# Attention and a two-layer feed-forward on one core: the GpSimd library, the first memsets and the first loads rearranged

## The chip, the core and the metric

The kernel runs on one core of one Trainium2 chip. The metric is the device time of one execution in microseconds (us), the median of several runs. The engines are called as in the profile: PE is TensorE, DVE is VectorE, ACT is ScalarE, POOL is GpSimd, and SP is the engine that issues the DMAs.

## The reference

Linear attention over 8 batches, 8 heads, 576 positions and 64 columns, then a feed-forward over the 4608 tokens with 512 columns:

```python
q_s = np.exp(q - np.max(q, axis=-1, keepdims=True))
q_s = q_s / (np.sum(q_s, axis=-1, keepdims=True) + 1e-09)
k_s = np.exp(k - np.max(k, axis=2, keepdims=True))
k_s = k_s / (np.sum(k_s, axis=2, keepdims=True) + 1e-09)
kv = np.einsum('bhsd,bhse->bhde', k_s, v)
attn = np.einsum('bhsd,bhde->bhse', q_s, kv)
x = attn.transpose(0, 2, 1, 3).reshape(B * S, H * D)
h = x @ w_in                        # w_in  512 x 2048, float64
g = h * (1.0 / (1.0 + np.exp(-1.702 * h)))
out = (g @ w_out).astype(np.float32)  # w_out 2048 x 512, float64
```

The maximum of k runs over the positions, which lie across the partitions; the maximum of q runs along a row.

## The kernel before

The 4608 tokens are 12 blocks (t) of 384. For each block the kernel makes x from the attention, and then for each of 16 slices j of the hidden dimension PE runs g1 (12 matmuls, `L585`), ACT the activation, and PE g2 (9 matmuls, `L617`). The weights arrive as 64-bit words, and `conv_w` turns each of the 32 weight tiles (wi0 to wi15, wo0 to wo15) into a high and a low part, once: two instructions on ACT (`L243`, `L256`) and four on DVE (`L247`, `L251`, `L252`, `L262`), some 2.5 us of DVE a tile. Blocks 0 and 1 run interleaved, while the weights are still being turned.

The attention of batch b starts with `k_max`: DVE takes the maximum over the chunks that one partition holds (`L378`, `L379`, `L380`, the last with the 64 tail positions), and POOL takes it across the partitions (`L384`, one PARTITION_ALL_REDUCE for each group of heads). Then `k_sub` subtracts it on DVE (`L398`, `L401`) and ACT takes the exponential; `kv_pair` multiplies with v on PE (`L441`, `L442`). `q_soft` is the softmax of q (`L479` to `L489`); `q_tr` transposes it on PE with the matrix `ident`, `x_pair` gives x. Batches 0 and 1 have two groups of four heads, later batches four of two.

All DMAs of loads stand in one queue, SP's, in the order batch 0's k, tail, k, q, q, eight of v, then wi0 and wo0, then batch 1, then the other weights. Eight semaphores are shared by them in turn, so that a DMA is issued when the eighth before it has landed. Tiles of batches 0 and 1 (ek, ev, eq, et) lie in buffers that the late weights take over. A `Plan` sorts all operations into one order for each engine from ranks and estimated costs; each engine then works through its own list in order.

Before all this, POOL clears or fills tiles with memsets, makes `ident` (a memset and an AFFINE_SELECT, lines of masks.py), and runs one PARTITION_ALL_REDUCE on 64 columns of a tile mx, `warm`, `L197`. The second group's maxima are written to the same tile mx by `L379`. The AFFINE_SELECT and the PARTITION_ALL_REDUCE belong to code libraries that the program loads into POOL; the loads are instructions in POOL's list.

Of the kernel before, what the change touches and what calls it, by code (L numbers as in the profile page):

```python
# [14 lines left out]
ALU = mybir.AluOpType  # L15
# [83 lines left out]
def dve(n, psum=False):  # L99
    return 0.15 + n / 960  # L100
# [7 lines left out]
def efficient_attention_then_gelu_ffn(  # L108
# [25 lines left out]
    SM = 512  # L134
    CM = SM // P
# [10 lines left out]
    def sb(name, shape, dtype=F32, tag=None):  # L146
        return const.tile(shape, dtype, name=name, tag=tag or name)
# [14 lines left out]
    m1_ = sb("m1", [P, 2 * 4 * D])  # L162
    tail = [(sb(f"kl{i}", [P, H, D]), sb(f"vl{i}", [P, H, W])) for i in range(1)]

    for t in kvn:
        nc.gpsimd.memset(t, 0.0)
    make_identity(nc, ident)
    for t in vt_:
        nc.gpsimd.memset(t[:, :, :, D:W], 1.0)

    def zero_tail(kl, vl):
        nc.gpsimd.memset(kl[ST:P], 0.0)
        nc.gpsimd.memset(vl[ST:P], 0.0)
# [5 lines left out]
    def early(tag, name, shape):
        return sb(name, shape, tag=tag)  # L180

    ek, ev, eq, etail = {}, {}, {}, {}
    for b in range(2):
        for gr in range(2):
            ek[b, gr] = early(f"wo{15 - 4 * b - gr}", f"ek{b}{gr}", [P, CM, 4, D]), f"wo{15 - 4 * b - gr}"
            ev[b, gr] = early(f"wo{13 - 4 * b - gr}", f"ev{b}{gr}", [P, 4, CM, W]), f"wo{13 - 4 * b - gr}"
            eq[b, gr] = early(f"wi{15 - 2 * b - gr}", f"eq{b}{gr}", [P, C, 4, D]), f"wi{15 - 2 * b - gr}"
            nc.gpsimd.memset(ev[b, gr][0][:, :, :, D:W], 1.0)
    et = early("wi11", "et", [P, H * (D + W)])
    etail[0] = (  # L190
        et[:, : H * D].rearrange("p (h d) -> p h d", h=H),
        et[:, H * D : H * (D + W)].rearrange("p (h d) -> p h d", h=H),
    ), "wi11"
    zero_tail(*etail[0][0])

    def warm():
        nc.gpsimd.partition_all_reduce(mx_[0][:, 0], mx_[0][:, 0], P, bass_isa.ReduceOp.max)  # L197

    nc.gpsimd.memset(mx_[0][:, 0], 0.0)
    plan.add("POOL", 6.0, (), (("mx", 0),), -1000, warm)  # L200

    wi = [[None] * NJ for _ in range(2)]
    wo = [[None] * NJ for _ in range(2)]
# [71 lines left out]
    def bc(a, n):  # L275
        return a.unsqueeze(len(a.shape)).broadcast_to([*a.shape, n])
# [23 lines left out]

    def load_k(b, i, rank):
        n = group(b)
        if b < 2:
            t, tag = ek[b, i]
            key = (tag, 0)
        else:
            t, key = kt_[i % 2], ("kt", i % 2)
        kbuf[b, i] = t, key
        hs = slice(n * i, n * (i + 1))

        def run():
            nc.sync.dma_start(  # L312
                out=t, in_=k[b, hs, 0:SM, :].rearrange("h (p c) d -> p c h d", c=CM)
            )

        plan.add("SP", plan.ISSUE, (), (key,), rank, run, size=n * SM * D * 4)

    def load_v(b, i, rank):
        n = group(b)
        if b < 2:  # L320
            t, tag = ev[b, i]
            key = (tag, 0)
        else:
            t, key = vt_[i % 2], ("vt", i % 2)
# [19 lines left out]

    def load_q(t, i, rank):
        n = group(t)
        if t < 2:
            qt, tag = eq[t, i]
            key = (tag, 0)
        else:  # L350
            qt, key = qt_[i % 2], ("qt", i % 2)
        qbuf[t, i] = qt, key
        hs = slice(n * i, n * (i + 1))

        def run():
            for b, s0, p0, p1 in parts(t):
                nc.sync.dma_start(  # L357
                    out=qt[p0:p1], in_=q[b, hs, s0 : s0 + (p1 - p0) * C, :].rearrange("h (p c) d -> p c h d", c=C)
                )

        plan.add("SP", plan.ISSUE * len(parts(t)), (), (key,), rank, run, size=n * TB * D * 4)

# [27 lines left out]
    def k_sub(b, i, rank):  # L390
        n = group(b)
        t, key = kbuf[b, i]
        kl, _, (lkey, _) = tbuf[b]
        mx, M = maxes[b, i]
        hs = slice(n * i, n * (i + 1))

        def run():
# [10 lines left out]
        plan.add("DVE", dve(n * CM * D) + dve(n * D), (key, M, lkey), (key, L), rank, run)  # L408
# [90 lines left out]
    def q_tr(t, hp, rank):  # L499
# [152 lines left out]
    def at(rank, f, *a):  # L652
        tasks.append((rank, len(tasks), f, a))
# [37 lines left out]
    attend(1, 1, 0.4, 0.1)  # L691
    for j in range(NJ):
# [67 lines left out]
```

## Time and profile before

| | us |
|---|---|
| median of 3 runs | 939.67 (lowest 938.83, highest 940.52) |
| profiled execution, its own time | 938.21 |
| span of its trace, first to last instruction | 936.4 |
| PE busy | 895.0 (96% of the span) |
| DVE busy | 410.2 (44%) |
| ACT busy | 508.5 (54%) |
| POOL busy | 28.0 (3%) |

Times in the trace count from the span's start. The profiled execution takes 1.8 us more than its span. An engine's share over the whole span is an average: the first 75 us look different from the rest.

### The profile page before, as it was taken

To read this page: it belongs to the slowest core of one execution; us is meant where nothing else is said; L and a number is where in the kernel's file an instruction comes from. 1 tells how busy PE (TensorE), PEld (TensorE's weight loads), DVE (VectorE), ACT (ScalarE), POOL (GpSimd) and SP (SyncE) were. 2 spreads that over 40 slices of the span, in tenths; PEclk is the share of its full clock that TensorE was granted. 3 is DMA by queue.
4 is the path that set the end of the run, shared out by engine and by line. 5 is a ranking of instruction groups with operands and counts; after the bars stand their busy time and mean duration, and the time that the engine had idled before them with its cause. 6 is when DMAs were issued, how large, how long until landed. Compare 5 with 4: busy or idle time off the path is not lost.

```text
span 936.4 us, 12002 instructions
## 1 busy us (share of the span) xinstructions
PE 895.0 (96%) x4652; PEld 810.9 (87%) x4652; DVE 410.2 (44%) x904; ACT 508.5 (54%) x876; POOL 28.0 (3%) x50
## 2 busy tenths in 40 slices
PE   0689999999999999999999999999999999999998
PEld 0568999899999999999999999999999999999997
DVE  2999996174351551441562443342355243142111
ACT  1776767366483783553675566454478275352222
POOL 3000000000000000000000000000000000000000
PEclk9899999999999999999999999999999999999999
DMA  9998000030121130000230230000222110000000
GB/s 209 269 372 211 1 1 1 34 100 22 36 47 55 42 74 35 18 18 34 62 74 34 63 73 35 18 17 35 54 48 56 43 33 18 35 18 1 35 1 34
DMA packets 129241, 55.30 MB, mean 59 GB/s; under 512 B 114336, under 2 KB 122528, under 8 KB 129184
## 3 DMA queue, kind: packets, MB, share of 16 engines
q1 hardware_dynamic: 129184, 54.54, 23.2%
q8 instruction: 36, 0.59, 0.2%
q14 instruction: 21, 0.17, 0.1%
HBM read 45.09 MB, written 9.44 MB: 58 GB/s over the span
## 4 chain that ended last, share of the span: by engine, by line
PE 92%; SPq 4%; DMA 2%; DVE 1%; issue 0%; ACT 0%; DVEq 0%
PE bank L585 43%; PE bank L617 42%; PE bank L552 2%; PE bank L441 2%; PE bank L508 1%; SPq L329 1%; DMA raw<-in_moe_w_out 1%; DMA raw<-in_moe_w_in 1%; SPq L357 1%; SPq L293 1%; PE bank L442 1%; SPq L213 0%; DVE tmp L251 0%; DVE tmp L252 0%; SPq L312 0%; SPq L218 0%
## 5 line engine op out<-in xcount | busy, mean ns | idle before, releaser
L585 PE MATMUL bank<-xh,w 128*128 128x384 f32 x1536 | 429.5, 341 | 4.6 <-ACT w L256 2.7
L617 PE MATMUL bank<-w,gh 128*128 128x512 f32 x1152 | 364.1, 397 | 1.4 <-ACT gh L594 1.4
L585 PEld LDWEIGHTS bank<-xh,w 128*128 128x128 f32 x1536 | 282.1, 188 | 12.3 <-ACT w L256 3.3
L597 DVE TENSOR_TENSOR gl<-g,gh 128x384 fp32r<-128x384 f32 x192 | 106.8, 556 | 384.7 <-ACT gh L594 376.9
L585 PE MATMUL bank<-xl,w 128*128 128x384 f32 x768 | 259.6, 338 | 0.0
L591 ACT ACTIVATE g<-bank 128x384 f32<-128x384 f32 x192 | 94.3, 491 | 301.2 <-PE bank L585 300.1
L617 PEld LDWEIGHTS bank<-w,gh 128*128 128x128 f32 x1152 | 212.5, 188 | 35.8 <-ACT gh L594 1.8
L617 PE MATMUL bank<-w,gl 128*128 128x512 f32 x576 | 227.6, 395 | 3.0 <-DVE gl L597 3.0
L585 PEld LDWEIGHTS bank<-xl,w 128*128 128x128 f32 x768 | 144.6, 188 | 6.0 <-DVE xl L562 0.3
L617 PEld LDWEIGHTS bank<-w,gl 128*128 128x128 f32 x576 | 108.6, 188 | 29.0 <-DVE gl L597 4.1
L594 ACT CAST gh<-g 128x384 fp32r<-128x384 f32 x192 | 98.5, 513 | 6.2 <-PE bank L617 0.3
L591 ACT ACT_TABLE_LOAD x58 | 74.4, 1283 | 1.0
L384 POOL PARTITION_ALL_REDUCE mx<-mx x28 | 23.4, 834 | 712.3 <-DVE mx L380 712.3
L483 ACT ACT_TABLE_LOAD x33 | 42.3, 1283 | 0.6
L451 ACT ACTIVATE kvn<-bank,r 64x64 f32<-64x64 f32 x64 | 19.6, 307 | 27.9 <-DVE r L446 26.1
L441 PE MATMUL bank<-ev,ek 128*128 128x130 f32 x64 | 12.0, 346 | 23.4 <-ACT ek L404 22.9
L479 DVE TENSOR_REDUCE qm<-qt 128x6 f32<-128x384 f32 x40 | 21.9, 548 | 25.5 <-DMA qt<-in_q 25.0
L486 DVE TENSOR_REDUCE qm<-qt 128x6 f32<-128x384 f32 x40 | 22.0, 549 | 25.3 <-ACT qt L483 25.2
L404 ACT ACT_TABLE_LOAD x25 | 32.1, 1283 | 1.1 <-PEq L747 0.7
L441 PEld LDWEIGHTS bank<-ev,ek 128*128 128x128 f32 x64 | 11.0, 256 | 24.1 <-POOL mx L384 22.9
L559 ACT CAST xh<-bank 128x384 fp32r<-128x384 f32 x48 | 22.7, 475 | 12.7 <-PE bank L552 12.3
L562 DVE TENSOR_TENSOR xl<-bank,xh 128x384 fp32r<-128x384 f32 x48 | 26.1, 551 | 5.9 <-ACT xh L559 5.8
(73 smaller groups left out, 590.6 us busy)
## 6 DMA issues: line engine op xcount, KB each, us to landing
out<-tmp SPq DMA_DIRECT2D x36, 256.0 KB, 2.1
raw<-in_moe_w_in SPq DMA_DIRECT2D x16, 512.0 KB, 10.3
raw<-in_moe_w_out SPq DMA_DIRECT2D x16, 512.0 KB, 9.3
kt<-in_k SPq DMA_DIRECT2D x24, 256.0 KB, 3.5
vt<-in_v SPq DMA_DIRECT2D x48, 128.0 KB, 3.4
qt<-in_q SPq DMA_DIRECT2D x28, 192.0 KB, 3.0
qt<-in_q SPq DMA_DIRECT2D x24, 96.0 KB, 2.6
ek<-in_k SPq DMA_DIRECT2D x4, 512.0 KB, 6.0
```

The costliest lines, as they stand in the source:

```text
L384: nc.gpsimd.partition_all_reduce(flat, flat, P, bass_isa.ReduceOp.max)
L404: nc.scalar.activation(t, t, AF.Exp)
L441: nc.tensor.matmul(pk[:, :w], kt[:, c, loc, :], vt[:, loc, c, :], start=c == 0, stop=False)
L483: nc.scalar.activation(qt, qt, AF.Exp)
L486: nc.vector.tensor_reduce(out=m, in_=qt, axis=AX.X, op=ALU.add)
L559: nc.scalar.copy(xh, px[:, :TB])
L562: nc.vector.tensor_tensor(out=xl, in0=px[:, :TB], in1=xh.bitcast(F32), op=ALU.subtract)
L585: nc.tensor.matmul(ph, wi[w][j][:, c, :], x[:, c, :], start=c == 0 and i == 0, stop=c == KC - 1 and i == 2,)
L591: nc.scalar.activation(gt, ph, AF.Gelu_apprx_sigmoid)
L594: nc.scalar.copy(gh, gt)
L597: nc.vector.tensor_tensor(out=gl, in0=gt, in1=gh.bitcast(F32), op=ALU.subtract)
L617: nc.tensor.matmul(po[c], x[:, cs], wo[w][j], start=j == 0 and i == 0, stop=j == NJ - 1 and i == 2)
```

## The change

Four things are changed, all in the first microseconds. The all-reduce that makes POOL load its library works on a tile of its own, `first`, and stands at the head of POOL's list. `ident` is made behind the two all-reduces of batch 0. All other memsets at the start are issued by DVE. The k and q of batch 0 are loaded with a head's rows of one partition together: runs of 1 KB (k, 4 rows of 256 bytes) and 768 bytes (q, 3 rows) in place of 256 bytes, into tiles with the head ahead of the chunk; the subtraction of k and the last step of q's softmax write into second tiles (em, en) in the old order of dimensions. For these, other buffers of late weights are taken: batch 0 now holds those of wi5 to wi10 and wo5 to wo9, batch 1 those of wi14, wi15 and wo12 to wo15.

```diff
+    first = sb("first", [P, D])
+    nc.vector.memset(first, 0.0)
+    nc.gpsimd.partition_all_reduce(first, first, P, bass_isa.ReduceOp.max)
     for t in kvn:
-        nc.gpsimd.memset(t, 0.0)
-    make_identity(nc, ident)
+        nc.vector.memset(t, 0.0)
...
-        nc.gpsimd.memset(kl[ST:P], 0.0)
+        nc.vector.memset(kl[ST:P], 0.0)
...
-            ek[b, gr] = early(f"wo{15 - 4 * b - gr}", f"ek{b}{gr}", [P, CM, 4, D]), f"wo{15 - 4 * b - gr}"
...
+        ek[0, gr] = early(f"wi{5 + gr}", f"ek0{gr}", [P, 4, CM, D], 0)
+        em[0, gr] = early(f"wo{5 + gr}", f"em0{gr}", [P, CM, 4, D], 0)
+        eq[0, gr] = early(f"wi{7 + gr}", f"eq0{gr}", [P, 4, C, D], 0)
+        en[0, gr] = early(f"wo{7 + gr}", f"en0{gr}", [P, C, 4, D], 0)
+        ev[0, gr] = early(f"w{'io'[gr]}9", f"ev0{gr}", [P, 4, CM, W], 0)
...
-    def warm():
-        nc.gpsimd.partition_all_reduce(mx_[0][:, 0], mx_[0][:, 0], P, bass_isa.ReduceOp.max)
-
-    nc.gpsimd.memset(mx_[0][:, 0], 0.0)
-    plan.add("POOL", 6.0, (), (("mx", 0),), -1000, warm)
+    plan.add("POOL", 7.0, (), ("first",), -1000, lambda: None)
...
-            nc.sync.dma_start(
-                out=t, in_=k[b, hs, 0:SM, :].rearrange("h (p c) d -> p c h d", c=CM)
-            )
+            if b == 0:
+                nc.sync.dma_start(
+                    out=t.rearrange("p h c d -> p h (c d)"),
+                    in_=k[b, hs, 0:SM, :].rearrange("h (p c) d -> p h (c d)", c=CM),
+                )
...
+        tv = t.rearrange("p h c d -> p c h d") if b == 0 else t
...
-            nc.vector.tensor_tensor(out=m1, in0=t[:, 0:2], in1=t[:, 2:4], op=ALU.max)
+            nc.vector.tensor_tensor(out=m1, in0=tv[:, 0:2], in1=tv[:, 2:4], op=ALU.max)
...
+        if b == 0:
+            src = t.rearrange("p h c d -> p c h d")
+            t, key = kbuf[b, i] = em[b, i]
...
-                out=t, in0=t, in1=mx.unsqueeze(1).broadcast_to([P, CM, n, D]), op=ALU.subtract
+                out=t, in0=src, in1=mx.unsqueeze(1).broadcast_to([P, CM, n, D]), op=ALU.subtract
...
-            nc.vector.tensor_tensor(out=qt, in0=qt, in1=bc(m, D), op=ALU.mult)
+            nc.vector.tensor_tensor(out=dst, in0=qt, in1=bc(m, D), op=ALU.mult)
...
-        plan.add("PE", 0.35, (key,), (PB,), rank, run)
+        plan.add("PE", 0.35, (key, "ident"), (PB,), rank, run)
...
+    at(-57.9, lambda rank: plan.add("POOL", 8.0, (("mx", 0), ("mx", 1)), ("ident",), rank, lambda: make_identity(nc, ident)))
     attend(0, 0, -60, 1)
```

POOL's list before, from its last memset on; an ISA row without a tile is the load of a library, one with mx is an all-reduce:

```order
L199 MEMSET mx_100 128x64
masks.py:199 ISA
masks.py:199 AFFINE_SELECT ident<-ident 128x128
L174 MEMSET vl_104 128x8
L174 MEMSET et 128x8
L197 ISA
L197 ISA mx_100<-mx_100 128x64
L384 ISA mx_101<-mx_101 128x256
L384 ISA mx_100<-mx_100 128x256
```

POOL's list of the change, from its start (behind four memsets of constants) to batch 1's first all-reduce:

```order
L168 ISA
L168 ISA first<-first 128x64
L390 ISA mx_101<-mx_101 128x256
L390 ISA mx_100<-mx_100 128x256
masks.py:197 MEMSET ident 128x128
masks.py:199 AFFINE_SELECT ident<-ident 128x128
L390 ISA mx_101<-mx_101 128x256
```

Of the two library loads one is left, it stands first, and the AFFINE_SELECT has none of its own; the 14 memsets ahead of the loads are gone from there.

DVE's list before, from its start to the first subtraction (ek_116 and ek_120 are the two groups of batch 0's k, m_102 the tile between, mx_101 and mx_100 their maxima):

```order
L378 TENSOR_TENSOR m_102<-ek_116 128x512
L379 TENSOR_TENSOR mx_101<-m_102 128x256
L380 TENSOR_TENSOR mx_101<-mx_101,et 64x256
L378 TENSOR_TENSOR m_102<-ek_120 128x512
L379 TENSOR_TENSOR mx_100<-m_102 128x256
L380 TENSOR_TENSOR mx_100<-mx_100,et 64x256
L398 TENSOR_TENSOR ek_116<-ek_116,mx_101 128x1024
```

The same stretch of the change (ek_115 and ek_125 are the groups; eight memsets of the start stand ahead of these rows):

```order
L199 MEMSET ev_122 128x16
L199 MEMSET ev_129 128x16
L199 MEMSET ev_132 128x16
L175 MEMSET et 64x512
L176 MEMSET et 64x520
L177 MEMSET vl_104 128x8
L384 TENSOR_TENSOR m_102<-ek_115 128x512
L177 MEMSET et 128x8
L385 TENSOR_TENSOR mx_101<-m_102 128x256
L386 TENSOR_TENSOR mx_101<-mx_101,et 64x256
L384 TENSOR_TENSOR m_102<-ek_125 128x512
L408 TENSOR_TENSOR em_116<-ek_115,mx_101 128x1024
```

DVE has 15 memsets more, 14 of them ahead of its first maximum, and keeps the order of the rest up to the conversion of the weights of slice 8; behind it the softmax of block 2's q moves some 60 rows back. PE's list is the same row for row but for the tiles' names. SP's list has the same order through wo5; of the later weights some change places.

## Rows read from the trace of the kernel before

**Rows 1.** Busy time of each engine, granted clock and DMA in three stretches.
```profile
20.50:74.50 54.00, 37.39 (x184) 30.32 (x184) 50.81 (x100) 37.66 (x74) 4.01 (x3) 0.91 1.15 308
74.50:78.00 3.50, 3.01 (x9) 3.01 (x10) 3.43 (x7) 1.86 (x3) 0.00 (x0) 0.54 0.97 243
78.00:150.00 72.00, 72.00 (x363) 65.43 (x363) 66.72 (x122) 48.47 (x86) 0.17 (x1) 1.00 0.17 44
```
Columns: stretch and its length, then PE, PEld, DVE, ACT and POOL busy us (with instructions), PE's granted clock, DMA share, GB/s.

**Rows 2.** Chain that ended last, 38 to 79 us: start, us, what.
```profile
38.45 11.10 DMA raw<-in_moe_w_out
...
74.33 0.61 DVE w L262
...
74.99 3.45 PE bank L585 x10
```

**Rows 3.** Timeline of POOL, 0 to 45 us: start, us, instruction, [idle before].
```profile
4.42 0.16 POOL L199 MEMSET mx<- 128x64 f32 x1
12.22 0.28 POOL masks.py:199 TENSOR_SCALAR_AFFINE_SELECT ident<-ident 128x128 f32<-128x128 f32 x1 [7.65 <-issue]
...
18.73 0.54 POOL L197 PARTITION_ALL_REDUCE mx<-mx  x1 [6.11 <-issue]
19.19 1.15 POOL L384 PARTITION_ALL_REDUCE mx<-mx  x1
20.79 1.89 POOL L384 PARTITION_ALL_REDUCE mx<-mx  x1 [0.45 <-DVE mx L380]
```

**Rows 4.** Timeline of DVE, 0 to 36 us.
```profile
6.25 0.69 DVE L378 TENSOR_TENSOR m<-ek 128x512 f32<-128x512 f32 x1 [6.25 <-DMA ek<-in_k]
...
7.44 0.42 DVE L380 TENSOR_TENSOR mx<-mx,et 64x256 f32<-64x256 f32 x1
10.07 0.69 DVE L378 TENSOR_TENSOR m<-ek 128x512 f32<-128x512 f32 x1 [2.21 <-DMA ek<-in_k]
19.31 0.86 DVE L379 TENSOR_TENSOR mx<-m 128x256 f32<-128x256 f32 x1 [8.54 <-POOL mx L197]
...
20.55 1.21 DVE L398 TENSOR_TENSOR ek<-ek,mx 128x1024 f32<-128x1024 f32 x1
...
33.97 0.41 DVE L247 TENSOR_SCALAR raw<-raw 128x512 uint32<-128x512 uint32 x1
34.41 0.69 DVE L251 SCALAR_TENSOR_TENSOR tmp<-tmp,raw 128x512 int32<-128x512 int32 x1
```

**Rows 5.** Timeline of SP: when a DMA was issued, and how long issuing took.
```profile
0.72 0.73 SPq L312 DMA_DIRECT2D ek<-in_k  x1
...
3.37 0.63 SPq L296 DMA_DIRECT2D et<-in_v  x1
...
15.52 0.62 SPq L213 DMA_DIRECT2D raw<-in_moe_w_in  x1
...
34.67 0.50 SPq L218 DMA_DIRECT2D raw<-in_moe_w_out  x1
35.22 0.43 SPq L213 DMA_DIRECT2D raw<-in_moe_w_in  x1
```

**Rows 6.** DMA issues, one window for each: KB, us to landing.
```profile
et<-in_v SPq DMA_DIRECT2D x1, 128.0 KB, 4.4
...
raw<-in_moe_w_in SPq DMA_DIRECT2D x1, 512.0 KB, 4.5
...
raw<-in_moe_w_out SPq DMA_DIRECT2D x1, 512.0 KB, 6.0
...
raw<-in_moe_w_in SPq DMA_DIRECT2D x1, 512.0 KB, 6.9
```

**Rows 7.** Timeline of ACT, 0 to 80 us.
```profile
28.46 0.64 ACT L243 ACTIVATE tmp<-raw 128x512 f32<-128x512 f32 x1
...
47.09 1.24 ACT L243 ACTIVATE tmp<-raw 128x512 f32<-128x512 f32 x2
53.08 0.48 ACT L529 COPY qTf<-bank 128x384 f32<-128x384 f32 x1 [4.75 <-PE bank L508]
```

More of the change, by code (lines that the diff above doesn't have):

```diff
@@ L163, in efficient_attention_then_gelu_ffn, with early @@
     tail = [(sb(f"kl{i}", [P, H, D]), sb(f"vl{i}", [P, H, W])) for i in range(1)]
+    first = sb("first", [P, D])
+    nc.vector.memset(first, 0.0)
+    nc.gpsimd.partition_all_reduce(first, first, P, bass_isa.ReduceOp.max)
     for t in kvn:
-        nc.gpsimd.memset(t, 0.0)
-    make_identity(nc, ident)
+        nc.vector.memset(t, 0.0)
     for t in vt_:
-        nc.gpsimd.memset(t[:, :, :, D:W], 1.0)
+        nc.vector.memset(t[:, :, :, D:W], 1.0)
     def zero_tail(kl, vl):
-        nc.gpsimd.memset(kl[ST:P], 0.0)
-        nc.gpsimd.memset(vl[ST:P], 0.0)
-        nc.gpsimd.memset(vl[:, :, D:W], 1.0)
+        nc.vector.memset(kl[ST:P], 0.0)
+        nc.vector.memset(vl[ST:P], 0.0)
+        nc.vector.memset(vl[:, :, D:W], 1.0)
     zero_tail(*tail[0])
[L179 to L184, printed above, removed]
-            ek[b, gr] = early(f"wo{15 - 4 * b - gr}", f"ek{b}{gr}", [P, CM, 4, D]), f"wo{15 - 4 * b - gr}"
[L186 to L189, printed above, removed]
+    held = {}
+    def early(tag, name, shape, batch):
+        held[tag] = batch
+        return sb(name, shape, tag=tag), (tag, 0)
+    ek, em, ev, eq, en, etail = {}, {}, {}, {}, {}, {}
+    for gr in range(2):
+        ek[0, gr] = early(f"wi{5 + gr}", f"ek0{gr}", [P, 4, CM, D], 0)
[3 more added lines that the diff above has]
+        ev[0, gr] = early(f"w{'io'[gr]}9", f"ev0{gr}", [P, 4, CM, W], 0)
+        ek[1, gr] = early(f"wo{14 + gr}", f"ek1{gr}", [P, CM, 4, D], 1)
+        eq[1, gr] = early(f"wi{14 + gr}", f"eq1{gr}", [P, C, 4, D], 1)
+        ev[1, gr] = early(f"wo{12 + gr}", f"ev1{gr}", [P, 4, CM, W], 1)
+        for b in range(2):
+            nc.vector.memset(ev[b, gr][0][:, :, :, D:W], 1.0)
+    et, _ = early("wi10", "et", [P, H * (D + W)], 0)
     etail[0] = (
@@ L192, in efficient_attention_then_gelu_ffn @@
         et[:, H * D : H * (D + W)].rearrange("p (h d) -> p h d", h=H),
-    ), "wi11"
+    ), "wi10"
     zero_tail(*etail[0][0])
-    def warm():
-        nc.gpsimd.partition_all_reduce(mx_[0][:, 0], mx_[0][:, 0], P, bass_isa.ReduceOp.max)
-    nc.gpsimd.memset(mx_[0][:, 0], 0.0)
-    plan.add("POOL", 6.0, (), (("mx", 0),), -1000, warm)
+    plan.add("POOL", 7.0, (), ("first",), -1000, lambda: None)
     wi = [[None] * NJ for _ in range(2)]
@@ L302, in load_k @@
         n = group(b)
[L303 to L307, printed above, removed]
+        t, key = ek[b, i] if b < 2 else (kt_[i % 2], ("kt", i % 2))
         kbuf[b, i] = t, key
@@ L311, in run @@
         def run():
-            nc.sync.dma_start(
-                out=t, in_=k[b, hs, 0:SM, :].rearrange("h (p c) d -> p c h d", c=CM)
-            )
+            if b == 0:
[3 more added lines that the diff above has]
+                )
+            else:
+                nc.sync.dma_start(out=t, in_=k[b, hs, 0:SM, :].rearrange("h (p c) d -> p c h d", c=CM))
         plan.add("SP", plan.ISSUE, (), (key,), rank, run, size=n * SM * D * 4)
@@ L319, in load_v @@
         n = group(b)
[L320 to L324, printed above, removed]
+        t, key = ev[b, i] if b < 2 else (vt_[i % 2], ("vt", i % 2))
         vbuf[b, i] = t, key
@@ L346, in load_q @@
         n = group(t)
[L347 to L351, printed above, removed]
+        qt, key = eq[t, i] if t < 2 else (qt_[i % 2], ("qt", i % 2))
         qbuf[t, i] = qt, key
@@ L356, in run @@
             for b, s0, p0, p1 in parts(t):
-                nc.sync.dma_start(
-                    out=qt[p0:p1], in_=q[b, hs, s0 : s0 + (p1 - p0) * C, :].rearrange("h (p c) d -> p c h d", c=C)
-                )
+                src = q[b, hs, s0 : s0 + (p1 - p0) * C, :]
+                if t == 0:
+                    nc.sync.dma_start(
+                        out=qt[p0:p1].rearrange("p h c d -> p h (c d)"),
+                        in_=src.rearrange("h (p c) d -> p h (c d)", c=C),
+                    )
+                else:
+                    nc.sync.dma_start(out=qt[p0:p1], in_=src.rearrange("h (p c) d -> p c h d", c=C))
         plan.add("SP", plan.ISSUE * len(parts(t)), (), (key,), rank, run, size=n * TB * D * 4)
@@ L395, in k_sub @@
         hs = slice(n * i, n * (i + 1))
+        src, skey = t, key
+        if b == 0:
+            src = t.rearrange("p h c d -> p c h d")
+            t, key = kbuf[b, i] = em[b, i]
         def run():
             nc.vector.tensor_tensor(
-                out=t, in0=t, in1=mx.unsqueeze(1).broadcast_to([P, CM, n, D]), op=ALU.subtract
+                out=t, in0=src, in1=mx.unsqueeze(1).broadcast_to([P, CM, n, D]), op=ALU.subtract
             )
@@ L407, in k_sub @@
         L = (lkey, i)
-        plan.add("DVE", dve(n * CM * D) + dve(n * D), (key, M, lkey), (key, L), rank, run)
+        plan.add("DVE", dve(n * CM * D) + dve(n * D), (skey, M, lkey), (key, L), rank, run)
         plan.add("ACT", act(n * CM * D) + act(n * D), (key, L), (key, L), rank, run_exp, table="exp")
@@ L474, in q_soft @@
         qt, key = qbuf[t, i]
-        m = qm[i % 2][:, :, 0:n]
         M = ("qm", i % 2)
+        if t == 0:
+            m = qm[i % 2].rearrange("p c h -> p (c h)").rearrange("p (h c) -> p h c", h=n)
+            qn, nkey = qbuf[t, i] = en[t, i]
+            dst = qn.rearrange("p c h d -> p h c d")
+        else:
+            m = qm[i % 2][:, :, 0:n]
+            dst, nkey = qt, key
         def run_m():
@@ L493, in q_soft @@
         plan.add("ACT", act(e), (key,), (key,), ranks[1], run_e, table="exp")
-        plan.add("DVE", 2 * dve(e) + 0.35, (key,), (key, M), ranks[2], run_s)
+        plan.add("DVE", 2 * dve(e) + 0.35, (key,), (nkey, M), ranks[2], run_s)
     nq = [0]
@@ L666, in efficient_attention_then_gelu_ffn @@
         for kind, d in (("wi", 0), ("wo", 0.5)):
-            n = int(kind == "wi" and j in (12, 13) or kind == "wo" and 8 <= j < 12)
-            late = kind == "wi" and j >= 11 or kind == "wo" and j >= 8
-            at((-45, 5)[n] if late else r + d, lambda _, kind=kind, j=j, r=r + d: load_w(j, kind, r))
+            late = {0: -45, 1: 5}.get(held.get(f"{kind}{j}"), r + d)
+            at(late, lambda _, kind=kind, j=j, r=r + d: load_w(j, kind, r))
     at(-83, load_k, 1, 0)
```

## The prediction

> **What bounds the kernel now.** I read the busy times by stretch first [rows 1]. From 78 to 150 us PE is busy for 72.00 of 72 us at the full clock (2.4 GHz). Of the 41.4 us that PE stands in the whole span (936.4 less 895.0 busy), 37.6 lie ahead of that stretch: 20.5 before the first subtraction, 16.6 from there to 74.5, 0.5 to 78. So from 78 on a change at the start can only move PE's work as a whole. From 20.5 to 74.5 DVE is busy for 50.81 of 54 us and PE for 37.39. The chain of waits says the same at the seam: a DVE instruction of the weights' conversion at 74.33 releases PE at 74.99, and PE keeps the chain from there on [rows 2]. So the end of the kernel hangs on when DVE gets through its list, and DVE has next to no holes from 20.5 on.
>
> Before 20.5 it has big ones. DVE does the maxima of batch 0's first group at 6.25, as soon as k lands, the first step of the second group at 10.07, and then sits for 8.54 us until 19.31, held by POOL's warm all-reduce at `L197`, which owns the tile that `L379` is to write [rows 4]. POOL's rows show why that all-reduce is late: after its last memset at 4.42 it stands for 7.65 us until the AFFINE_SELECT, and for another 6.11 us until the all-reduce at 18.73, with no instruction in the gaps [rows 3]. Those are the two library loads of POOL's list. The first real all-reduce begins at 19.19 and the first subtraction, `L398`, at 20.55. From that instruction on DVE's list runs as one block.
>
> **The change, part by part.** What counts is when the first subtraction (now `L408`) can start. It needs the first all-reduce, and it stands behind the second group's maxima in DVE's list.
>
> POOL: the one load that is left starts at about 0.72, when the lists begin [rows 5], in place of 4.58 (4.42 + 0.16 [rows 3]). The loads of before cost 6.11 and 7.65 us, and I keep both as bounds. The load ends at 6.8 to 8.4. The all-reduce on `first` delays the next one by 0.46 (18.73 to 19.19 [rows 3]), so POOL is ready at 7.3 to 8.85.
>
> DVE's memsets: the trace has no memset on DVE. Six of the 15 have 512 or 520 elements in a partition; the nearest rows are 0.41 us (`L247`, one input) and 0.69 us (`L251`) for 512 elements [rows 4], so 2.5 to 4.1 us. The nine small ones cost from nothing to 0.16 each, which is what POOL took for 64 columns [rows 3], so up to 1.4. Together they end between 3.2 and 6.2. They lie beside POOL's load and beside the first transfer. If this cover were gone they would cost what they last.
>
> The loads: the tail of v was issued at 3.37 and landed 4.4 later, at 7.8 [rows 5, 6]; the second group of k, behind it in the stream, released DVE at 10.07 [rows 4]. That is 2.27 us for 512 KB in runs of 256 bytes. A tile of w_out landed at 34.67 + 6.0 = 40.7, the next of w_in, 512 KB in runs of 1 KB, at 35.22 + 6.9 = 42.1 [rows 5, 6]: 1.45 us. So each k group saves 0.82 us (bounds: nothing and 0.82; I take 0.82, since the stream was full in both places). By bytes the two q of 384 KB save up to 0.61 each, together 2 x 0.82 + 2 x 0.61 = 2.86 us for everything that lands later. The first k then lands at 6.25 - 0.82 = 5.4, the second at 10.07 - 1.64 = 8.4.
>
> The sum: DVE starts the first maxima at about 5.7 (memsets or k, whichever is last). They took 7.44 + 0.42 - 6.25 = 1.61 us before, and one small memset stands between, so they are ready at 7.5. The first all-reduce starts at 7.5 to 8.85, lasts 1.15, and ends at 8.65 to 10.0. The second maxima run from 8.4 to 10.0. I take 10.1 for the first subtraction, with 0.1 for the handover: 20.55 - 10.1 = **10.45 us** earlier. The second all-reduce then runs from 10.1 to at most 12.0 (1.89 [rows 3]); `L408` of that group comes only after three more DVE instructions behind a 1.21 us one. `ident` is ready half a microsecond later, and PE first reads it behind the whole softmax of q.
>
> Does the block behind it follow by the full 10.45? Only if the transfers do. wi0 landed at 15.52 + 4.5 = 20.0 [rows 5, 6] and ACT used it at 28.46 [rows 7], 8.4 us later; with 2.86 earlier there are 11.3, enough. wo1 landed at 40.7 and is read by the second of two instructions that start at 47.09, at 47.7: 7.0 + 2.86 = 9.86, so 0.6 too late. Behind it ACT stands idle for 4.75 us, until 53.08 [rows 7], and this takes it up. Later tiles land every 1.4 us or so and cost DVE 2.5 us each, so their lead grows. I cost the exchange of buffers at nothing: batch 0's last reads of them come before the first g1, and SP comes to wi5 only after batch 1 and four slices of weights. The strided reads of k and writes of q cost nothing either: `L251`, which reads every second word, takes 0.69 us, as `L378` does on 512 packed elements [rows 4].
>
> The profiled execution of 938.21 (span 936.4 and 1.8 around it) becomes 927.8. It lies 1.5 under the median; the median of 939.67 becomes **929.2**.
>
> **A rule against it.** The all-reduce beside which DVE has little to do takes 1.15 us, and the one that runs while DVE subtracts takes 1.89 [rows 3, 4]. In the change the first all-reduce runs beside the second group's maxima. The Trainium skill, page "GPSIMD Engine Reference", section "Specifications", says that POOL shares its SBUF interfaces with VectorE and contends with instructions of VectorE that have two SBUF inputs; the 1.89 us agree with it. By it the gain is the 9.8 of the first rival below, by the 1.15 us the 10.45 above.
>
> **The rivals.**
> - *Contention*: the first all-reduce takes 1.89, from 8.85, and ends at 10.75; the gain is 9.8, **929.9**. For it speak the two durations; against it, that DVE's maxima start before the late end of the load and may be through. Chance 0.15.
> - *The 1 KB runs land no earlier* (the start, not the stream, sets the first landings): the second k at 10.07, its maxima at 11.7, gain 8.9, **930.8**. For it: the first landing came 5.5 us after its issue (0.72 to 6.25 [rows 4, 5]), far more than 2.27 us of data. Chance 0.12.
> - *The clock*: PE began its dense block at 0.54 of the clock, the lower of its two levels (1.2 GHz), for 3.5 us [rows 1], after a stretch in which PE stood for 16.6 us of 54. One such stretch more costs half of it, 1.75: **931.0**. The stretch falling away would give 927.5. Chance of one more 0.07; nothing in the change makes PE's holes longer.
> - *The transfers bound the start*: the chain of waits stands on a transfer of weights for 11.10 us from 38.45 [rows 2]. Then only the 2.86 us come, **936.8**. Against it speak DVE's 50.81 us of 54 and the leads above. Chance 0.05.
> - *The first load costs what both did*, 13.76, because something has to be fetched once whatever comes first: the first subtraction at 0.72 + 13.76 + 0.46 + 1.15 = 16.1, gain 4.45, **935.2**. Chance 0.05.
> - *Slower*: reading k across head and chunk slows DVE. The instructions that do it are two like `L378` (0.69) and two like `L398` (1.21), 3.8 us; beyond the 10.45 gained the kernel is slower by more than 0.2% (1.9 us) when they take over four times as long. That would give 941.6 or more. `L251` at every second word speaks against it. Chance 0.02.
> - *Nothing comes of it*, within 0.2%: some of the above together, 0.03.
>
> **How the numbers follow.** The likeliest case, 929.2, has 0.51. Its bounds: were the second k never late, POOL's early end of 8.65 would decide, gain 11.9, 927.8; the latest landing gives 930.8. The range takes in the case of the falling stretch at the low end and the late landing with one more low stretch at the other (939.67 - 8.9 + 1.75 = 932.5): 927.4 to 932.5, with about 0.85 in it. 0.2% is about what a measurement of this kernel can tell from no change. Faster by more has 0.95, within 0.03, slower 0.02.
>
> **What the profile would show.** POOL's first all-reduce at 6.8 to 8.4, with one gap ahead of it in place of two, and the AFFINE_SELECT right behind the second one of batch 0. DVE's first subtraction near 10.1, released by POOL or right behind its own maxima. The second k released at about 8.4. DVE as full as before between 10 and 64, and PE's dense block from about 64.5. It would be wrong if the gap ahead of the first all-reduce is over 10 us, if a DMA of weights ends a DVE or ACT wait of more than a microsecond between 10 and 64 us, or if the AFFINE_SELECT has a gap of its own that PE's transposes then wait for.

## The result and the profile after

The changed kernel takes 929.75 us, the median of four runs (929.56 to 930.13), against 939.51 for the kernel before beside it: 9.76 us less, a ratio of 0.9896 with an interval of 0.9879 to 0.9913 (8.2 to 11.4 us). Forecast were 929.2 and 10.45 less. The profiled execution takes 930.13, where 927.8 was forecast for it; its span is 928.4 us, 8.0 shorter than before.

POOL's timeline of the changed kernel, 1 to 13 us (start, us, instruction, [idle before and what ended it]):

```profile
1.02 0.52 POOL L168 PARTITION_ALL_REDUCE first<-first  x1 [0.58 <-DVE first L167]
7.02 1.06 POOL L390 PARTITION_ALL_REDUCE mx<-mx  x1 [5.47 <-DVE mx L386]
10.24 1.97 POOL L390 PARTITION_ALL_REDUCE mx<-mx  x1 [2.17 <-DVE mx L386]
12.09 0.27 POOL masks.py:197 MEMSET ident<- 128x128 f32 x1
12.44 0.29 POOL masks.py:199 TENSOR_SCALAR_AFFINE_SELECT ident<-ident 128x128 f32<-128x128 f32 x1
```

Both gaps of [rows 3] are gone, and so is the one that was to be left: the all-reduce that stands behind the library's load begins at 1.02 us, as soon as DVE has cleared its tile. The first real one waits for DVE's maxima, not for POOL.

DVE's timeline of the same kernel:

```profile
0.98 1.03 DVE L170 MEMSET kvn<- 128x512 f32 x2
...
4.71 0.07 DVE L177 MEMSET vl<- 128x8 f32 x1
5.32 0.69 DVE L384 TENSOR_TENSOR m<-ek 128x512 f32<-128x512 f32 x1 [0.55 <-DMA ek<-in_k]
...
8.55 0.69 DVE L384 TENSOR_TENSOR m<-ek 128x512 f32<-128x512 f32 x1 [1.62 <-DMA ek<-in_k]
...
10.08 1.21 DVE L408 TENSOR_TENSOR em<-ek,mx 128x1024 f32<-128x1024 f32 x1
11.21 0.82 DVE L411 TENSOR_TENSOR et<-et,mx 64x256 f32<-64x256 f32 x1
...
19.45 0.15 DVE L455 TENSOR_SCALAR r<-bank 128x1 f32<-128x1 f32 x1
...
23.47 0.16 DVE L455 TENSOR_SCALAR r<-bank 128x1 f32<-128x1 f32 x1 [1.10 <-PE bank L452]
...
27.16 0.16 DVE L455 TENSOR_SCALAR r<-bank 128x1 f32<-128x1 f32 x1 [0.38 <-PE bank L452]
...
31.82 0.68 DVE L384 TENSOR_TENSOR m<-ek 128x512 f32<-128x512 f32 x1
...
45.71 0.69 DVE L269 TENSOR_TENSOR w<-tmp,w 128x512 fp32r<-128x512 f32 x1 [0.83 <-ACT w L263]
```

The first subtraction, `L408`, starts at 10.08 in place of 20.55 [rows 4]: 10.47 us earlier. Then the lead shrinks. Four rows of the kernel before stand opposite:

```profile
29.92 0.15 DVE L445 TENSOR_SCALAR r<-bank 128x1 f32<-128x1 f32 x1
...
33.69 0.16 DVE L445 TENSOR_SCALAR r<-bank 128x1 f32<-128x1 f32 x1 [0.85 <-PE bank L442]
36.68 0.15 DVE L445 TENSOR_SCALAR r<-bank 128x1 f32<-128x1 f32 x1
41.20 0.69 DVE L378 TENSOR_TENSOR m<-ek 128x512 f32<-128x512 f32 x1
```

At 19.45 it is still 10.47 (29.92 before); at batch 1's first maxima, 31.82, it is 9.38 (41.20). What came between are mostly longer waits for PE. PE's timeline of the changed kernel shows why:

```profile
12.43 2.10 PE L451 MATMUL bank<-ev,em 128*128 128x130 f32 x8 [12.43 <-ACT em L414]
...
20.99 1.94 PE L451 MATMUL bank<-ev,em 128*128 128x130 f32 x8
...
25.84 1.06 PE L451 MATMUL bank<-ev,em 128*128 128x130 f32 x8
...
66.05 0.85 PE L601 MATMUL bank<-xh,w 128*128 128x384 f32 x2 [1.16 <-DVE w L269]
```

The same eight matmuls take 2.10 and 1.94 us up to 25 us and 1.06 from 25.84 on: PE ran at the lower of its two levels, 1.2 GHz, all the way from its first matmul to there. The dense block starts at 66.05, 8.94 earlier than in [rows 2], 1.5 later than forecast, and its first 3.4 us are at half the clock, as they were before [rows 1]. The windows of the changed kernel say the same (columns as in [rows 1]; ahead of 25.3 the clock column has no record, there the durations tell the level):

```profile
25.30:35.50 10.20, 6.84 (x35) 4.67 (x34) 9.09 (x18) 8.32 (x16) 1.06 (x1) 1.00 1.29 195
35.50:42.40 6.90, 5.14 (x17) 4.48 (x18) 6.59 (x13) 3.28 (x5) 1.06 (x1) 0.51 1.05 382
...
66.20:69.70 3.50, 3.50 (x12) 3.41 (x13) 3.33 (x7) 1.41 (x3) 0.00 (x0) 0.51 1.12 290
```

The kernel before has these low stretches too:

```profile
30.40:33.80 3.40, 3.40 (x16) 3.20 (x15) 2.44 (x6) 2.82 (x7) 0.00 (x0) 0.50 1.41 200
...
44.00:50.90 6.90, 4.26 (x13) 3.59 (x14) 6.73 (x12) 3.45 (x6) 1.08 (x2) 0.51 1.05 377
```

Its first three groups of eight matmuls take 2.07, 1.90 and 2.02 us as well (at 22.95, 25.25 and 31.13). The difference is when the clock rises. Before, it was up over PE's pause from 27.0 to 30.4, down again, and rose at 33.8; 10.47 us earlier would be 23.3, and in the changed kernel it was 25.3, 2 us later. The second low stretch ended at 50.9; 9.38 us earlier would be 41.5, and it was 42.4. At half the clock these delays are worth 1.0 and 0.4 us, which is about what the lead lost.

From the dense block to the span's end the lead goes from 8.94 to 8.0 (PE's last matmul still leads by 8.5); where this last part went was not pursued.

### The profile page after: what moved, and what is told of

It reads as the page before. It is cut to its first block, busy times and chain, and to the rows that moved or that the text cites. A ratio compares the mean times of both kernels' runs of the same rounds, so it can differ in the third digit from the quotient of the medians.

```text
span 928.4 us, 12001 instructions
## 1 busy us (share of the span) xinstructions
PE 897.1 (97%) x4652; PEld 812.4 (88%) x4652; DVE 413.9 (45%) x919; ACT 509.2 (55%) x876; POOL 24.8 (3%) x35
## 4 chain that ended last, share of the span: by engine, by line
PE 93%; SPq 3%; DVE 2%; ACT 1%; DMA 0%; issue 0%; DVEq 0%; ACTq 0%
PE bank L633 43%; PE bank L601 43%; PE bank L451 3%; PE bank L568 2%; PE bank L524 1%; SPq L332 1%; PE bank L452 1%; SPq L363 1%; SPq L300 1%; DMA ev<-in_v 0%; DVE tmp L258 0%; DVE tmp L259 0%; DVE w L269 0%; SPq L358 0%; DVE raw L254 0%
## 5 line engine op out<-in xcount | busy, mean ns | idle before, releaser
L250 ACT ACTIVATE tmp<-raw 128x512 f32<-128x512 f32 x32 | 21.4, 674 | 7.9 <-DVE w L269 7.5
L451 PE MATMUL bank<-vt,kt 128*128 128x130 f32 x192 | 25.4, 274 | 0.0
```

Of the source, the lines that this page charges most:

```text
L451: nc.tensor.matmul(pk[:, :w], kt[:, c, loc, :], vt[:, loc, c, :], start=c == 0, stop=False)
```

## The experiments

All were timed beside the kernel before. Three questions: which part of the change brings the gain, why POOL's library cost nothing, and where the microsecond behind the first subtraction went.

**The other library left behind** (`lib_left`):

```diff
         for n in plan.order():
             plan.ops[n][4]()
+        nc.gpsimd.tensor_tensor(out=first, in0=first, in1=first, op=ALU.add)
```

> The changed kernel with one more GpSimd instruction at the very end of POOL's list (an addition of the tile `first` to itself, which nothing reads), which needs the other library; POOL then ends each execution with that other library loaded. Theory A (a library stays loaded from one execution to the next, and the changed kernel, which ends on the same library that it begins with, has nothing to load): the first all-reduce, which began at 1.02 us in the changed kernel, now begins between 6.8 and 8.8 us behind a gap of 6.1 to 7.7 us, the lengths of the two gaps in the kernel before. The first real all-reduce starts then or at 7.0, whichever is later, ends by 10.0, and the first subtraction stays near 10.1 to 10.4 because the second group's k and its maxima hold it: time 929.75 to 930.3. Theory B (the first load of a kernel costs nothing, whatever was loaded before): the all-reduce stays at 1.02 us, the time too. Theory C (POOL ready at 1.5 us in place of 7.3 to 8.85 is what the gain rests on): first subtraction 1 us or more later, time 930.8 or more.

928.97 us, ratio 0.9889 (0.9875 to 0.9902), 0.8 us under the expected 929.75 to 930.3, which the interval reaches. Its timelines of POOL and of DVE:

```profile
7.65 0.54 POOL L168 PARTITION_ALL_REDUCE first<-first  x1 [7.22 <-issue]
8.11 1.15 POOL L390 PARTITION_ALL_REDUCE mx<-mx  x1
```
```profile
8.82 0.69 DVE L384 TENSOR_TENSOR m<-ek 128x512 f32<-128x512 f32 x1 [2.25 <-DMA ek<-in_k]
...
10.35 1.21 DVE L408 TENSOR_TENSOR em<-ek,mx 128x1024 f32<-128x1024 f32 x1
```

Theory A holds. The added instruction starts at 752.97 us behind a gap of 6.90 us of its own, so it does need the other library, and it brings 7.22 us back to the start of the list: a library stays loaded over executions, the kernel before had to swap twice because it used two, and the changed kernel loads none. The load is hidden: the second group of k and its maxima hold the subtraction in any case.

**Identity first, two loads** (`ident_first`):

```diff
-    nc.vector.memset(first, 0.0)
-    nc.gpsimd.partition_all_reduce(first, first, P, bass_isa.ReduceOp.max)
+    make_identity(nc, ident)
+    nc.gpsimd.partition_all_reduce(first, ident[:, 0:D], P, bass_isa.ReduceOp.max)
```

> The changed kernel with the identity made first on POOL, as in the kernel before, and the warm all-reduce behind it (it reads the identity, so that it can't go ahead of it); memsets stay on VectorE and the 1 KB runs stay. Theory (the two library loads on POOL's list are what held the first subtraction): two gaps come back, 7.65 and 6.11 us by the kernel before, the warm all-reduce begins at 14.5 to 15.5 us, the first real one ends at 16.2 to 17.2, the first subtraction comes at 16.3 to 17.3 in place of 10.08, 6.2 to 7.2 us later: time 935.5 to 937.5 (one stretch of the lower clock more or less is 1 us of that). Rival (the earlier landings of k and q bring the gain): no more than 1 us above 929.75. Rival (only one of the loads costs time when the memsets are gone): 929.75 to 932.

935.83 us, 0.9963 (0.9949 to 0.9977). POOL's and DVE's timelines:

```profile
8.52 0.28 POOL masks.py:199 TENSOR_SCALAR_AFFINE_SELECT ident<-ident 128x128 f32<-128x128 f32 x1 [7.59 <-issue]
14.68 0.54 POOL L168 PARTITION_ALL_REDUCE first<-ident  x1 [5.88 <-issue]
```
```profile
16.33 1.64 DVE L408 TENSOR_TENSOR em<-ek,mx 128x1024 f32<-128x1024 f32 x1 [6.07 <-POOL mx L390]
```

As expected: the subtraction comes 6.25 us later than in the changed kernel, and 6.1 us are lost at the end.

**POOL's old list with the new loads, and with the old ones** (`pool_old`, `pool_old_256`): memsets and identity back on POOL ahead of the all-reduce, in the second also 256-byte runs.

```diff
-    nc.vector.memset(first, 0.0)
-    nc.gpsimd.partition_all_reduce(first, first, P, bass_isa.ReduceOp.max)
...
+    make_identity(nc, ident)
...
-        nc.vector.memset(kl[ST:P], 0.0)
+        nc.gpsimd.memset(kl[ST:P], 0.0)
...
+    nc.gpsimd.memset(first, 0.0)
+    nc.gpsimd.partition_all_reduce(first, first, P, bass_isa.ReduceOp.max)
     plan.add("POOL", 7.0, (), ("first",), -1000, lambda: None)
```

> The changed kernel with all 15 memsets and the identity on POOL ahead of the warm all-reduce, as in the kernel before; the 1 KB runs, the separate target tiles and the warm all-reduce on its own tile stay. Theory (POOL's list sets the first subtraction): POOL's two gaps stand as before, the warm all-reduce begins at 18 to 19 us, the first subtraction at 20 to 20.6 though the k groups land at 5.3 and 8.5: time 939 to 940, the change's loads are worth nothing alone. Rival (the loads carry a part of the gain by themselves): 936.8 or less, by the 2.5 us that the later tiles land earlier.

> POOL's list as in the kernel before (memsets and the identity first, two library loads) with the 256-byte runs as well; of the change only the separate target tiles and the warm all-reduce's own tile are left. With 1 KB runs this list had gaps of 9.63 and 8.58 us and 942.40 us in all. Theory (a library load shares the way from memory with the transfers, and the denser 1 KB runs push weights and batch 1 under the second load): the gaps are back near 7.65 and 6.11, the warm all-reduce at 18.3 to 19.2, first subtraction at 20 to 20.8, time 938.5 to 940. Rival (a load's length depends on something in POOL's list itself, such as the memsets or the tile of the warm all-reduce): gaps stay over 8 us each, time over 941.5.

942.40 us, 1.0035 (1.0023 to 1.0048), and 939.09, 1.0002 (0.9993 to 1.0011). POOL's timeline of the first, then of the second:

```profile
14.21 0.28 POOL masks.py:199 TENSOR_SCALAR_AFFINE_SELECT ident<-ident 128x128 f32<-128x128 f32 x1 [9.63 <-issue]
...
23.19 0.54 POOL L207 PARTITION_ALL_REDUCE first<-first  x1 [8.58 <-issue]
```
```profile
12.29 0.28 POOL masks.py:199 TENSOR_SCALAR_AFFINE_SELECT ident<-ident 128x128 f32<-128x128 f32 x1 [7.72 <-issue]
...
18.77 0.54 POOL L207 PARTITION_ALL_REDUCE first<-first  x1 [6.09 <-issue]
```

My number for `pool_old` was a miss, on the far side of both theories: under POOL's old list the new loads of k and q make the kernel 3 us slower. With the same list, only the runs changed, the two library loads are 1.9 and 2.5 us longer (one trace of each). Step by step: from `pool_old_256` to `ident_first` the memsets go to DVE, the first load starts at 0.93 in place of 4.58, and 1 KB runs come in (3.3 us at the end, together); from there to the changed kernel both loads go (6.1).

**256-byte runs alone** (`runs_256`): the loads of batch 0's k and q as before, the rest of the change kept.

```diff
-            if b == 0:
-                nc.sync.dma_start(
-                    out=t.rearrange("p h c d -> p h (c d)"),
-                    in_=k[b, hs, 0:SM, :].rearrange("h (p c) d -> p h (c d)", c=CM),
-                )
-            else:
-                nc.sync.dma_start(out=t, in_=...)
+            nc.sync.dma_start(out=t, in_=k[b, hs, 0:SM, :].rearrange("h (p c) d -> p c h d", c=CM))
```

> The changed kernel with the first batch's k and q loaded in runs of 256 bytes into tiles laid out as in the kernel before; POOL's and VectorE's part and the separate target tiles stay. Theory (behind POOL's repair the landing of the second k group sets the first subtraction): that group lands at about 10.05 in place of 8.53, the first subtraction comes at 11.6 to 11.8 in place of 10.08, everything behind it follows, the weights of the first slice land at about 20.0 and hold ScalarE for up to half a microsecond: time 931.0 to 932.0, 1.2 to 2.2 us above 929.75. Rival (POOL's libraries alone bring the gain, the runs are hidden): within 0.4 us of 929.75. Rival (the strided reads cost what the runs bring): within 0.4 us too, but then with the first subtraction 1.5 us later and shorter DVE instructions.

929.54 us, 0.9895 (0.9881 to 0.9908): no loss to be seen, though the intervals reach over 1 us to either side, so that the 1.2 us of the theory's low end are not quite excluded. DVE's timeline:

```profile
9.94 0.69 DVE L372 TENSOR_TENSOR m<-ek 128x512 f32<-128x512 f32 x1 [2.39 <-DMA ek<-in_k]
...
11.47 1.21 DVE L395 TENSOR_TENSOR em<-ek,mx 128x1024 f32<-128x1024 f32 x1
...
32.07 0.68 DVE L372 TENSOR_TENSOR m<-ek 128x512 f32<-128x512 f32 x1
```

The landing and the subtraction are as late as the theory has it, by 1.39 us each, but batch 1 begins only 0.25 us after 31.82. Its dense block starts at 65.71, even 0.34 us before the changed kernel's. PE's low stretch ended at 24.4 in this profile, 0.9 us before the changed kernel's 25.3, and that took the lateness up; why it ended earlier the run does not show. Hence the next four.

**The changed kernel again, and matmuls of zeros for PE's pauses** (`after_again`, `warm_9`, `warm_fill`, `warm_256`). The zeros go into a bank that is overwritten before it is read; `warm_fill` has 9, 7, 2 and 4 of them in four places, and `warm_256` is `warm_fill` with the 256-byte runs.

```diff
+    def fill(n):
+        for _ in range(n):
+            nc.tensor.matmul(
+                bank[6], kvn[1][:, 0, :], kvn[1].rearrange("p a b -> p (a b)"), start=True, stop=True
+            )
...
+        fill(9)
         for n in plan.order():
...
+            if (b, hp) == (0, 1):
+                fill(7)
```

> The changed kernel once more, as the base for the three kernels beside it: 929.0 to 930.2, first subtraction at 10.0 to 10.4 us. If the moments at which the granted clock changes are not tied to the program, the stretch of the lower clock (0.5) that ended at 42.36 us ends elsewhere by up to a few microseconds in this profile.

> The changed kernel with nine matmuls of zeros (128x512 f32) at the head of PE's list, into a bank that nothing reads before it is overwritten; PE is then busy from about 3 to 10 or 12 us, before its first real matmul at 12.43. Theory (after the first subtraction the gain was eaten by PE at 0.5 of the clock between 12.4 and 25.3 us): the first eight kv matmuls take about 1.06 us in place of 2.10, but PE then stands until the q softmax is through at about 19.6, and the clock may fall in that pause; so 928.8 if it holds, 929.8 if it falls for the transposes and the third pair. Rival (something other than PE's clock delays VectorE and ScalarE between 22 and 28 us): the kv matmuls are shorter, the waits on PE of 1.10 and 0.38 us on VectorE stay, 929.7.

> The kernel with the nine matmuls of zeros and 13 more of the same kind in PE's next three pauses: seven behind the second kv pair, two behind the first slice's first product, four inside its second. Theory (the clock): transposes and the third kv pair run at the full clock, VectorE's waits of 1.10 and 0.38 us and ScalarE's of 1.76 and 0.55 us at that place shrink to 0.3 or less each, VectorE's first instruction for batch 1 comes at 30.6 to 31.0 in place of 31.82, the 0.5 stretch from 35.54 to 42.36 is gone and the wait of 0.83 for the converted weights with it; PE's dense block begins 1.0 to 1.6 us earlier, 928.0 to 928.8. Rival (transfers hold the stretch, the clock only seems to): the first slices' weights end new waits of ScalarE of the same length, 929.4 or more. Rival (the added matmuls themselves delay PE): transposes later than 19.7, slower than 930.

> The same matmuls of zeros with the first batch's k and q in 256-byte runs. Without them the 256-byte runs started the first subtraction 1.39 us later and yet cost nothing at the end (929.54). Theory (the slow clock hid them, since PE's low stretch ended at about the same time in both): with PE at the full clock the lateness stays, 1.0 to 1.5 us above the kernel with the same matmuls and 1 KB runs. Rival (the lateness is swallowed by some other wait that both kernels share, a transfer of weights or batch 1's loads): within 0.4 us of it.

929.43 (0.9894), 929.85 (0.9899), 928.94 (0.9889) and 933.06 (0.9928, 0.9911 to 0.9944). `after_again` repeats the time, but not each row: its second group of k landed at 9.03 in place of 8.55 and the first subtraction came at 10.55, outside the 10.0 to 10.4 expected. DVE's first row of batch 1:

```profile
32.22 0.68 DVE L384 TENSOR_TENSOR m<-ek 128x512 f32<-128x512 f32 x1
```

So two executions of one kernel differ by 0.4 to 0.5 us here, and batch 1 of `runs_256` (32.07) is no later than this one. Its low stretch ended at 42.7 in place of 42.4, too little to say what ties the clock. In `warm_9` the first pairs run in 1.16 and 1.06 us, but the clock falls in the pause behind them and the third pair takes 1.94 again, the branch without a gain. `warm_fill` is inconclusive as a time; in its five executions the span falls as the mean granted clock rises: spans of 924.5, 925.5, 927.2, 928.5 and 929.2 us at a mean granted clock of 0.999, 0.997, 0.995, 0.992 and 0.992. Its seven matmuls were too many: its PE timeline:

```profile
14.99 6.17 PE L211 MATMUL bank<-kvn 128*128 128x512 f32 x14
21.66 1.06 PE L457 MATMUL bank<-ev,em 128*128 128x130 f32 x8
```

They end at 21.16, behind the 19.68 at which the transposes start in the changed kernel. `warm_256` loses 4.1 us against `warm_fill`, where 1.0 to 1.5 were expected: a miss. Part of it may be this chain, which began 2.1 us later there; that was not tried by itself.

**The same, cut to the pauses, up to 66 us, and with both sizes of runs** (`fill_all`, `fill_256`): 9, 4, 1 and 3 matmuls at these places, and ten half as long ones in six later places, as

```diff
+            if (t, j) in ((0, 1), (0, 3)):
+                fill(2, 256)
             for c in range(KC):
                 for i, (w, x) in enumerate(((0, xh), (0, xl), (1, xh))):
+                    if t == 0 and (c, i) == (0, 2) and j in (1, 2, 3):
+                        fill(1 + (j == 3), 256, 7 - n % 2)
```

> The changed kernel with matmuls of zeros in PE's pauses up to 66 us, in sizes cut to the pauses of its own trace (nine of 128x512 f32 at the head, four behind the second kv pair, where seven made the transposes 1.5 us late, one behind the first slice's first product, three inside its second, and ten of 128x256 in five later pauses of 0.7 to 1.7 us). Theory (PE's 0.5 stretches cost the missing part of the gain): hardly a 0.5 stretch is left between 13 and 70 us, VectorE's waits on PE between 20 and 30 us stay under 0.5 us, the dense block begins at 64.0 to 65.0 at the full clock in place of 66.1 to 66.4 at half of it, so 2.5 to 4 us less than the changed kernel: 925.5 to 927.0. Rival (the weights' transfers bind as soon as the clock does not): dense block no earlier than 65.5 with a wait on a transfer ahead of it, 928 or more.

> The kernel with the right-sized matmuls of zeros (925.81 us, ratio to before 0.9862) with the first batch's k and q in 256-byte runs. Theory (the 1 KB runs' 1.4 us are hidden only while PE's low clock swallows them): first subtraction at 11.4 to 11.7 in place of 10.52, VectorE's first instruction for batch 1 at 30.8 to 31.4 in place of 29.88, the dense block that much later, ratio 0.987 to 0.988, 0.8 to 1.6 us more. Rival (the runs are hidden in any case): batch 1 begins within 0.4 us of 29.88, ratio 0.986. Of the 4 us by which the same edit slowed the kernel with the longer chain of zeros, the theory puts the rest on that chain, which then began 2.1 us later and held the transposes.

`fill_all` takes 925.81 us, 0.9862 (0.9849 to 0.9876): 12.7 us under the kernel before, 3 under the changed one by the ratios, the best of all. Its windows and one row of PE:

```profile
12.80:43.00 30.20, 25.20 (x126) 17.26 (x127) 29.10 (x56) 20.42 (x38) 2.42 (x3) 1.00 1.11 240
43.00:46.40 3.40, 3.40 (x12) 3.21 (x11) 3.33 (x10) 2.94 (x8) 0.00 (x0) 0.50 1.06 379
...
66.20:69.70 3.50, 3.50 (x19) 3.12 (x19) 3.33 (x6) 2.06 (x5) 0.00 (x0) 1.00 1.07 353
```
```profile
64.53 0.62 PE L614 MATMUL bank<-xh,w 128*128 128x384 f32 x2 [0.28 <-DVE w L274]
```

From 12.8 on one low stretch is left where the changed kernel has three; the dense block starts at 64.53, where the prediction wanted it, and at the full clock. `fill_256` takes 928.18 us, 0.9889 (0.9873 to 0.9906), above the upper end of the 0.987 to 0.988 expected. DVE's timelines of `fill_all` and of `fill_256`, then two rows of PE of `fill_256`:

```profile
10.52 1.21 DVE L413 TENSOR_TENSOR em<-ek,mx 128x1024 f32<-128x1024 f32 x1
...
29.88 0.68 DVE L389 TENSOR_TENSOR m<-ek 128x512 f32<-128x512 f32 x1
```
```profile
11.20 1.21 DVE L400 TENSOR_TENSOR em<-ek,mx 128x1024 f32<-128x1024 f32 x1
...
31.39 0.68 DVE L377 TENSOR_TENSOR m<-ek 128x512 f32<-128x512 f32 x1
```
```profile
15.75 1.94 PE L443 MATMUL bank<-ev,em 128*128 128x130 f32 x8
...
64.70 0.61 PE L601 MATMUL bank<-xh,w 128*128 128x384 f32 x2 [0.29 <-DVE w L274]
```

With PE filled, `fill_256` is 0.68 us late at the subtraction (11.20, under the 11.4 to 11.7 expected) and 1.51 at batch 1. The second number is not the runs alone: in this profile PE was at half the clock for a stretch from 15.8 on that `fill_all` does not have (1.94 us for the eight matmuls that take 1.06 there), and the zeros behind it held the transposes (22.0 against 20.1). And the lateness is gone at the dense block: 64.70 against 64.53, where 0.8 to 1.6 us were expected, and the two profiled spans are 925.2 and 925.0. The medians still lie 2.4 us apart, and the four executions of each do not overlap (924.73 to 926.79 against 926.97 to 928.20). So the times speak for the 1 KB runs in this kernel, but no row shows where they bring the end forward; that stays open, and in the changed kernel no gain from them was seen.

**Memsets back on POOL** (`memset_pool`): 14 of them, around the all-reduce on `first`.

```diff
-        nc.vector.memset(kl[ST:P], 0.0)
+        nc.gpsimd.memset(kl[ST:P], 0.0)
...
```

> The changed kernel with 14 of its 15 memsets back on POOL, around and behind the warm all-reduce; the library, the identity's place and the loads stay. Theory (the memsets cost nothing on either engine as long as they end before the first k lands, at 5.3 us): POOL is through with them at about 5.5, the first real all-reduce starts at 7.0 as now, time within 0.5 us of the changed kernel (929.4 to 929.8). Rival (memsets on POOL hold up the first all-reduce): it starts at 8 us or later and the first subtraction later than 10.6, 930.5 or more.

927.76 us, 0.9885 (0.9871 to 0.9898), below the range by 1.6 us; the kernel before was lower there too (938.55), and the interval overlaps with the changed kernel's. The first real all-reduce starts at 6.89, the subtraction at 10.04: the memsets cost nothing that can be seen on either engine; on POOL they hold up a library that has to be loaded behind them, as in `pool_old_256`. Its profile shows one thing more. Two stretches of the windows, DVE's first row of batch 1, and the start of PE's dense block:

```profile
19.55:22.95 3.40, 3.31 (x16) 3.34 (x17) 2.60 (x8) 2.85 (x7) 0.00 (x0) 0.51 1.38 186
23.00:33.20 10.20, 7.99 (x40) 5.45 (x39) 9.48 (x21) 8.23 (x16) 0.83 (x1) 1.00 1.39 199
```
```profile
30.68 0.69 DVE L384 TENSOR_TENSOR m<-ek 128x512 f32<-128x512 f32 x1
```
```profile
64.36 1.01 PE L601 MATMUL bank<-xh,w 128*128 128x384 f32 x2 [1.14 <-DVE w L269]
```

PE has the same list as in the changed kernel and starts it at the same 12.43, but its clock rises at 23.0 in place of 25.3, batch 1 begins 1.14 us earlier, and the dense block starts at 64.36, where the prediction wanted it, without any matmul of zeros. This execution took 927.78 us; 927.8 was the forecast for the changed kernel's. `fill_all`, timed beside the same executions of the kernel before, lies 2 us under `memset_pool`: its dense block starts at about the same time, but at the full clock (0.62 us for the two matmuls that take 1.01 here).

## Why the prediction was right, and where its steps were not

- *The first subtraction at 10.1*: 10.08, and by the mechanism that the prediction gave, the second group's landing (8.4 forecast, 8.55) and its maxima. First k 5.4 forecast, 5.32; memsets through between 3.2 and 6.2, 4.78; second all-reduce by 12.0, 12.21. The AFFINE_SELECT has no gap of its own.
- *The number* came nearer than the traces: the median is 0.55 us above its forecast, the profiled execution 2.3 above. Of the two profiled executions the one before lay 1.3 us under its median, the one after 0.4 over. That the median hit so closely is in part luck, since 1.5 us of the lead were lost on the way to the dense block in the trace.
- *POOL ready at 7.3 to 8.85* is the step that failed: 1.54. It took the remaining load at 6.11 to 7.65, as the two before. `lib_left` shows the price (7.22) and why it isn't paid. The forecast did not hang on it: with the 7.22 back, the time is the same.
- *1 KB runs save 0.82 us a group*: two groups gave 1.39 (9.94 in `runs_256` against 8.55), not 1.64. Over all the profiles the second group released DVE at 8.51 to 9.25 with 1 KB runs and at 9.66 to 10.07 with 256-byte runs, on average 1.1 us apart, so some 0.5 us a group. That they also bring forward the end did not show in the changed kernel (`runs_256`).
- *Does the block follow by the full 10.45?* The prediction looked to the transfers, and was right that they don't decide: the second of ACT's weights is late by 0.42 us, and ACT's next wait is for PE. What it passed over is PE's clock over the first products. Its rival "the clock" (0.07) had one more low stretch at the dense block. What happened is that the low stretches of before did not move forward with the work: the first ended 2 us late against it and cost 1.09 us by 31.82 (10.47 to 9.38), the next, 35.5 to 42.4, some 0.44 more (9.38 to 8.94, the 0.83 us wait at 45.71). `fill_all` wins 1.52 us up to the dense block (64.53 against 66.05) and starts that at the full clock; `memset_pool` wins as much to there by an earlier rise of the clock alone.
- *Contention* (0.15): the first real all-reduce took 1.06 us beside an idle DVE, the second 1.97 beside `L408` and `L411`, and `L411` 0.82 in place of 0.41. `L408` itself took 1.21 us beside the all-reduce and 1.22 at 13.81 without one. The effect is there but off the path, since DVE stood idle at the first. So far the trace agrees with the Trainium skill, page "GPSIMD Engine Reference", section "Specifications", that POOL shares its SBUF interfaces with VectorE and contends with instructions of two SBUF inputs. One reading of the prediction does not hold: beside the all-reduce of 1.15 us in [rows 4] DVE did work, at `L379`, which took 0.86 us at 19.31 and 0.43 at 6.98. Beside an idle DVE the price is 1.06.
- *Strided reads and other buffers at nothing*: `L384` takes 0.69 and `L408` 1.21 us, as `L378` and `L398` in [rows 4]; `pool_old_256` has the second tiles and is as fast as before.

## What to carry to other kernels

Look for what a program leaves loaded: a kernel that uses one library of POOL finds it there at the next execution, one that uses two pays for both each time, and if nothing else holds the work behind them that is time lost. When a start is moved forward, ask what PE's clock does with it: about a microsecond of lead was lost here where PE still ran at 1.2 GHz, and matmuls of zeros cut to its pauses brought 2 to 3 us. Cut them too long and they become the wait.

## What was not expected of the hardware

- A library of POOL stays loaded from one execution to the next: the all-reduce behind its load began at 1.02 us, and at 7.65 when the execution before had ended on the other one.
- Such a load is longer with 1 KB runs than with 256-byte runs under the same list: 9.63 and 8.58 us against 7.72 and 6.09. With 1 KB runs, but begun 3.7 and 5.8 us earlier (`ident_first`), the loads took 7.59 and 5.88, so the runs alone do not set the length. That it depends on which transfers a load meets, because it shares a way with them, is the argued cause, and was not tried by itself.
- The moments at which PE's clock changes do not follow from PE's list: with the same list and start of PE it rose at 25.3 us in the changed kernel's profile and at 23.0 in `memset_pool`'s. The Trainium skill, page "TensorE: Matmul & The Clock Gate", section "What's actually happening", says that the slow start differs from run to run; these rows agree. In `warm_fill` the spread between executions goes with the clock (its spans above), but not in every kernel: the executions of the kernel before with a mean clock of 0.994 have spans of 937.4 to 938.9 us, those with 0.992 have 935.7 to 938.3.
